# A 2D Fourier transform and an MLP in one kernel: the sequence transform multiplies plain float32 instead of high and low halves

## The chip, the cores and the metric

The kernel runs on one core of a Trainium2 chip. Its engines work side by side, each through a queue of its own: TensorE (PE, matrix products; its weight loads are shown apart as PEld), VectorE (DVE), ScalarE (ACT), GpSimd (POOL) and SyncE (SP, which here only issues transfers). Products land in PSUM, an accumulator memory, and VectorE or ScalarE read it out into SBUF, the working memory. The metric is device time of one execution in microseconds; less is better.

## The reference

```python
def _attn_ref(x):                       # x: (8, 3008, 256) float32
    X = np.fft.fft(x, axis=1)
    X = np.fft.fft(X, axis=2)
    return X.real.astype(np.float32)

def _moe_ref(x, w_in, w_out, s, b):     # x: (24064, 256), w_in: (256, 2048), w_out: (2048, 256)
    h = x @ w_in
    r = np.maximum(h, 0.0)
    g = s * (r * r) + b
    return (g @ w_out).astype(np.float32)
```

The real part of a 2D transform of each of eight samples goes, row by row, through a two-layer MLP whose activation is the square of a ReLU.

## The kernel before

**Two ways to multiply.** Most products take float32r operands, a rounded form of float32. The kernel gets its accuracy back by splitting a float32 operand into a high half (rounded to float32r by ScalarE, "h") and a low half (the rest, by VectorE or GpSimd, "l") and adding three products: high by high, low by high, high by low. A plain float32 product needs no halves; the kernel uses it where it folds the feature transform into `w_in` (L337, L345). In the trace every float32 matmul stands as two records, each with its own weight load.

**The sequence transform** (`transform(su, ph)`, L567 to L669) runs once for each sample `su` and each parity `ph`. VectorE folds the rows of x into `cs` (`load`), builds small inputs `lf` (`leaves_x`, `leaves_y`), and TensorE multiplies them by tables `dft_sb` in four pairs (leaf 0, 2, 4, 6; `pair`, L598). ScalarE makes the high halves `fh` (L576), VectorE the low halves `fl` (L579). Of a pair the result stands in an `ab` buffer of PSUM. From the second sample on, a product with the high data runs over both table halves at once (192 columns) and one with the low data over 96, so that two halves of the sum stand side by side in PSUM: VectorE copies one out (L605), adds the other (L606), and then works on from SBUF. For sample 0 the three products accumulate in PSUM, and ScalarE copies one result out (L618, `two`) so that a VectorE operation has one operand from PSUM and the other from SBUF. Sums and differences (`both`, L610 and L611) follow, and `store` splits the outcome into `spec_h` (ScalarE, L563) and `spec_l` (GpSimd, L565).

**The MLP** works in blocks of 502 columns, three for each sample, and 16 steps for each block: 384 steps. The first layer of a step is six matmuls into an `ab` buffer (L678). VectorE reads it with three operations (L680 to L682) into `h`, ScalarE applies ReLU and square and casts the result to `gh` (L683, L684, L691), GpSimd makes `gl` (L694). The second layer is twelve matmuls (L711) into four `po` banks.

**The shared buffers.** `ps_ab` has two buffers, used by the first layer and by the pairs alike. A matmul group that wants a buffer waits until the last reader of the buffer's former content is through.

**What sets the order.** The program is written out one short letter at a time and every engine keeps that order (`_in_order`, L236). START (L50) covers the weights, sample 0 and the transforms of sample 1; BATCH (L59) covers 48 steps of one sample and the two transforms of the next, and is run six times with transforms. In BATCH `L` is a first layer with its VectorE, ScalarE and GpSimd work, `S` a second layer, `l` a half of a load, `v` and `o` the next piece of the transforms of parity 0 and 1. A piece ends at a `yield`: the matmuls of a pair are one piece, and reading them out is the next. Whatever a piece issues on ScalarE thus stands behind the ReLU, the square and the cast of every `L` before it.

The row of x at feature 128 is handled apart (`nyquist`, L477): the same tables with 16 weight columns.

Of the kernel before, what the change touches and what calls it, by code (L numbers as in the profile page):

```python
# [37 lines left out]

# [4 lines left out]
COPIES_ON_SCALAR = ()  # L43
# [14 lines left out]
)  # L58
BATCH = (  # L59
# [3 lines left out]
)  # L63

# [62 lines left out]
def _dft_tables():  # L127
# [91 lines left out]
def _lay_out_x(x):  # L219

    rows, swap = _rows()
    padded = np.zeros((NB, S + 1, D), np.float32)
    padded[:, :S] = x
    first = np.arange(P)
    second = np.concatenate([[0], D - np.arange(1, P)])
    order = np.stack([np.concatenate([first, second]), np.concatenate([second, first])])
    xq = np.ascontiguousarray(padded[:, rows[..., None], order[swap]])  # L230
# [20 lines left out]
def kernel(ctx: ExitStack, tc: tile.TileContext, xq, xn, dft, turn, feat, w_in, w_out, s, b, out):  # L251
# [109 lines left out]
    dft_sb = const.tile([R, 2, 2, 8, 2, NL], F32R, name="dft_sb")  # L361
# [49 lines left out]
    def nyquist(ph, t, room, room_r):  # L411

        if ph == 0:
# [23 lines left out]
        def table(leaf, count):  # L437

            return lambda part: dft_sb[:, ph, 0, leaf, part].rearrange("p (r g) -> p r g", r=4)[
                :, :, None].broadcast_to((R, 4, count, G))  # L440

        def pairs(leaf):
            return lambda part: dft_sb[:, ph, 0, leaf, part].rearrange("p (r m) -> p r m", r=2)

        def one(leaf):
            return lambda part: dft_sb[:, ph, 0, leaf, part]

        def twice(moving, *shape):
            return lambda part: moving(part)[:, None].broadcast_to((R, 2) + shape)
# [24 lines left out]
        for i, (dst, leaf, signs, moving) in enumerate(work):  # L474
            h, l = (e_[:, leaf, signs:signs + 2].rearrange("p n b -> p (n b)") for e_ in (eh, el))
            for n, (st, part) in enumerate(((h, 0), (h, 1), (l, 0))):
                nc.tensor.matmul(dst, st, moving(part), start=i == n == 0, stop=i == len(work) - 1 and n == 2)  # L477
# [89 lines left out]
    def transform(su, ph):  # L567
# [4 lines left out]
        def halve(src):  # L572
            fh = fold.tile([R, 4, 2 * P], F32R, name="fh")
            fl = fold.tile([R, 4, 2 * P], F32R, name="fl")
            for at, v in src:
                nc.scalar.copy(fh[:, at], v)  # L576
            yield fh, fl
            for at, v in src:
                sub(fl[:, at], v, fh[:, at].bitcast(F32))  # L579
            yield  # L580

        def pair(leaf, f):

            fh, fl = f
            parts = 1 if su == 0 else 2
            ps = two_banks()[:, :, :2 * parts * NL].rearrange("p k (i h g) -> p k i h g", i=2, h=parts)
            for kind in range(2):
                at = slice(kind * P, (kind + 1) * P)
                for i in range(2):
                    tab = dft_sb[:, ph, kind, leaf + i]  # L590
                    h, l = (v[:, leaf % 4 + i, at] for v in (fh, fl))
                    if su == 0:
                        work = (ps[:, kind, i, 0], h, tab[:, 0]), (ps[:, kind, i, 0], h, tab[:, 1])
                    else:
                        work = (ps[:, kind, i], h, tab),
                    work += (ps[:, kind, i, parts - 1], l, tab[:, 0]),
                    for n, (dst, st, moving) in enumerate(work):
                        nc.tensor.matmul(dst, st, moving, start=n == 0, stop=n == len(work) - 1)  # L598
# [7 lines left out]
            add(l, l, ps[:, :, :, 0])  # L606
            return t, l
# [28 lines left out]
        t, l = yield from pair(2, f)  # L636
# [9 lines left out]
        lf = small.tile([R, 4, 2 * P], F32, name="lf", tag="tmp")  # L646
# [5 lines left out]
        g = halve([(slice(0, 4), lf)])  # L652
        f = next(g)
        yield
        next(g)
# [159 lines left out]
    def second():  # L818
# [11 lines left out]
        "n": nyquist(0, t_ny, room, room_r), "m": nyquist(1, t_ny, room, room_r),  # L830
# [62 lines left out]
```

## Time and profile before

| | |
|---|---|
| time, median of 3 runs (lowest to highest) | 1713.73 us (1713.5 to 1713.96) |
| span of the profiled execution, first to last instruction | 1711.8 us |
| what lies around that span, by the median | 1.9 us |
| PE busy, share of the span | 1675.4 us, 98% |
| PEld busy | 1382.8 us, 81% |
| DVE busy | 1395.7 us, 82% |
| ACT busy | 1284.3 us, 75% |
| POOL busy | 934.7 us, 55% |
| mean granted TensorE clock | 0.997 |

The engines overlap, so the busy times do not add up to the span. The engine with the largest share, here TensorE, sets the time only as long as nothing makes it wait; what an operation of another engine costs is decided by whether TensorE is held by it.

### The profile page before, as it was taken

How to read it: one execution, taken by the hardware profiler on the slowest of the kernel's cores; microseconds unless marked ns; L12 is line 12 of the kernel's file. 1: busy time of each engine (PE TensorE's matmuls, PEld its weight loads, DVE VectorE, ACT ScalarE, POOL GpSimd, SP SyncE). 2: the span in 40 equal slices, each digit the busy share in tenths (PEclk: the TensorE clock that was granted, in tenths of full speed). 3: DMA queues.
4: the chain of work that ended last, by engine and by line, in shares of the span. 5: the costliest groups of instructions: out<-in, count | busy, mean ns of one | idle time of the engine just before them, and what ended most of it. 6: DMA issues, size and time to landing. Idle time of an engine off the chain costs nothing.

```text
span 1711.8 us, 21668 instructions
## 1 busy us (share of the span) xinstructions
PE 1675.4 (98%) x7585; PEld 1382.8 (81%) x7585; DVE 1395.7 (82%) x2119; ACT 1284.3 (75%) x1357; POOL 934.7 (55%) x562
## 2 busy tenths in 40 slices
PE   4899999999999999999999999999999999999998
PEld 3678888788888888888888888888888888888887
DVE  7888989898778978799787997879878897875454
ACT  3877777677787777877877778777878777787776
POOL 5545555555555455655556556555565555565554
PEclk9899999999999999999999999999999999999999
DMA  7421201120001100021000200002000110000000
GB/s 184 111 63 59 67 19 31 31 74 30 1 30 46 60 31 2 29 77 29 31 7 34 77 25 25 31 25 71 23 18 30 44 43 31 1 31 29 2 24 25
DMA packets 25570, 68.56 MB, mean 40 GB/s; under 512 B 4915, under 2 KB 9875, under 8 KB 25366
## 3 DMA queue, kind: packets, MB, share of 16 engines
q1 hardware_dynamic: 24934, 64.83, 12.3%
q0 software_dynamic: 528, 2.36, 0.6%
q8 instruction: 59, 0.97, 0.2%
q14 instruction: 49, 0.40, 0.1%
HBM read 42.45 MB, written 24.73 MB: 39 GB/s over the span
## 4 chain that ended last, share of the span: by engine, by line
PE 92%; DVE 5%; ACT 1%; DMA 1%; issue 1%; POOL 0%; SPq 0%; DVEq 0%; ACTq 0%; POOLq 0%
PE po L711 59%; PE ab L678 29%; PE ab L598 3%; DVE h L680 1%; DVE h L681 1%; PE ab L337 1%; DMA raw<-in_w_in 1%; DVE h L682 1%; PE ab L477 0%; DVE xt L511 0%; DVE cs L516 0%; POOL gl L694 0%; ACT h L684 0%; ACT h L683 0%; DVE fl L579 0%
## 5 line engine op out<-in xcount | busy, mean ns | idle before, releaser
L694 POOL TENSOR_TENSOR gl<-h,gh 128x1004 fp32r<-128x1004 f32 x373 | 818.1, 2193 | 708.2 <-ACT gh L691 486.3
L683 ACT ACTIVATE h<-h 128x1004 f32<-128x1004 f32 x384 | 400.3, 1042 | 351.3 <-DVE h L682 340.1
L711 PE MATMUL po<-gh,wo_h 128*128 128x502 f32 (+1 forms) x1536 | 480.5, 393 | 0.2
L711 PE MATMUL po<-gl,wo_h 128*128 128x502 f32 (+1 forms) x1536 | 475.5, 391 | 0.5 <-POOL gl L694 0.4
L711 PE MATMUL po<-gh,wo_l 128*128 128x502 f32 (+1 forms) x1536 | 475.6, 391 | 0.0
L680 DVE SCALAR_TENSOR_TENSOR h<-ebc,wny,ab 128x502 f32<-128x502 f32 x384 | 281.3, 733 | 236.5 <-PE ab L678 224.0
L684 ACT ACTIVATE h<-h 128x1004 f32<-128x1004 f32 x384 | 401.2, 1045 | 12.2
L691 ACT CAST gh<-h 128x1004 fp32r<-128x1004 f32 x384 | 397.4, 1035 | 12.6 <-PE po L711 0.3
L711 PEld LDWEIGHTS po<-gl,wo_h 128*128 128x128 f32 x1536 | 290.5, 189 | 61.4 <-POOL gl L694 2.0
L711 PEld LDWEIGHTS po<-gh,wo_l 128*128 128x128 f32 x1536 | 289.1, 188 | 61.3
L711 PEld LDWEIGHTS po<-gh,wo_h 128*128 128x128 f32 x1536 | 286.7, 189 | 60.0 <-DVE o L734 3.3
L678 PE MATMUL ab<-spec_h,wd_h 128*128 128x502 f32 x768 | 303.5, 395 | 7.0 <-ACT spec_h L563 3.7
L678 PE MATMUL ab<-spec_h,wd_l 128*128 128x502 f32 x768 | 300.3, 391 | 0.0
L678 PE MATMUL ab<-spec_l,wd_h 128*128 128x502 f32 x768 | 299.6, 390 | 0.4 <-POOL spec_l L565 0.4
L682 DVE TENSOR_TENSOR h<-h,ab 128x502 f32<-128x502 f32 x384 | 260.6, 679 | 13.3
L681 DVE TENSOR_TENSOR h<-h,ab 128x502 f32<-128x502 f32 x384 | 260.2, 678 | 13.2
L678 PEld LDWEIGHTS ab<-spec_h,wd_h 128*128 128x128 f32 x768 | 145.9, 190 | 42.5 <-DVE h L682 9.0
L678 PEld LDWEIGHTS ab<-spec_l,wd_h 128*128 128x128 f32 x768 | 146.0, 190 | 29.6 <-POOL spec_l L565 0.9
L678 PEld LDWEIGHTS ab<-spec_h,wd_l 128*128 128x128 f32 x768 | 144.9, 189 | 30.1
L598 PE MATMUL ab<-dft_sb,fh 96*128 96x192 f32 (+1 forms) x288 | 65.8, 306 | 18.4 <-ACT fh L576 18.4
L734 DVE TENSOR_SCALAR o<-po,sb_s,bias 128x502 f32<-128x502 f32 (+1 forms) x95 | 69.2, 792 | 9.8 <-PE po L711 9.8
L511 DVE TENSOR_TENSOR xt<-xt 96x512 f32<-96x512 f32 x56 | 72.6, 1296 | 0.0
(101 smaller groups left out, 950.8 us busy)
## 6 DMA issues: line engine op xcount, KB each, us to landing
xt<-in_xq SPq DMA_DIRECT2D x64, 384.0 KB
out<-o SPq DMA_DIRECT2D x46, 502.0 KB
raw<-in_w_in SPq DMA_DIRECT2D x8, 512.0 KB
raw<-in_w_out SPq DMA_DIRECT2D x8, 512.0 KB
ebc<-e_dram SPq DMA_DIRECT2D x16, 251.0 KB
dft_sb<-in_dft POOLq DMA_DIRECT2D x2, 576.0 KB, 10.1
dft_sb<-in_dft POOLq DMA_DIRECT2D x1, 1152.0 KB, 7.3
ebc<-e_dram SPq DMA_DIRECT2D x8, 126.0 KB
```

The source lines that it names most:

```text
L511: add(t[:, 0::2], t[:, 0::2], t[:, 1::2])
L598: nc.tensor.matmul(dst, st, moving, start=n == 0, stop=n == len(work) - 1)
L678: nc.tensor.matmul(ps[:, kind], w[:, kind, fj], m[:, kind], start=i == 0, stop=i == 2)
L680: nc.vector.scalar_tensor_tensor(h[:, 0], ebc, wny[:, j:j + 1], ps[:, 0], op0=ALU.mult, op1=ALU.add)
L681: sub(h[:, 1], h[:, 0], ps[:, 1])
L682: add(h[:, 0], h[:, 0], ps[:, 1])
L683: nc.scalar.activation(h, h, AF.Relu)
L684: nc.scalar.activation(h, h, AF.Square)
L691: nc.scalar.copy(gh[:, :, :NT], h)
L694: engine.tensor_sub(gl[:, :, :NT], h, gh[:, :, :NT].bitcast(F32))
L711: nc.tensor.matmul(po[2 * pm + dh][:, :n], l[:, j, dh * P:(dh + 1) * P], r[:, pm, :n], start=start and first, stop=stop and last,)
L734: nc.vector.tensor_scalar(dst, src, *args, ALU.mult, ALU.add)
```

## The change

The tables are stored once, as float32, and the pairs and the Nyquist rows multiply float32 data by float32 tables: one matmul where there were two (samples 1 to 7) or three (sample 0 and Nyquist rows). The halves `fh`, `fl`, `eh`, `el` and the pieces that made them are gone, and with them one or two letters of each transform in START and BATCH (all other letters keep their order). The copy and the sum of PSUM halves (L605, L606) are gone too. Every sample now reads a pair the way sample 0 did: `two` copies one of the two results out on ScalarE, and `both` reads the other from PSUM. That holds for two pairs of parity 0 (leaf 0 and 6) and all four of parity 1; the other two pairs of parity 0 are read by `both` directly. The `ab` buffer of a pair is therefore free once the ScalarE copy and the two VectorE operations behind it are through. `lf` moves to a pool with one buffer.

```diff
-    return np.ascontiguousarray(np.stack([hi, v - hi], axis=4))
+    return np.ascontiguousarray(out.astype(np.float32))
...
-    dft_sb = const.tile([R, 2, 2, 8, 2, NL], F32R, name="dft_sb")
+    dft_sb = const.tile([R, 2, 2, 8, NL], F32, name="dft_sb")
...
-            h, l = (e_[:, leaf, signs:signs + 2].rearrange("p n b -> p (n b)") for e_ in (eh, el))
-            for n, (st, part) in enumerate(((h, 0), (h, 1), (l, 0))):
-                nc.tensor.matmul(dst, st, moving(part), start=i == n == 0, stop=i == len(work) - 1 and n == 2)
+            nc.tensor.matmul(
+                dst, signed[:, leaf, signs:signs + 2].rearrange("p n b -> p (n b)"), moving, start=i == 0,
+                stop=i == len(work) - 1,
+            )
...
-        def halve(src):
-            fh = fold.tile([R, 4, 2 * P], F32R, name="fh")
-            fl = fold.tile([R, 4, 2 * P], F32R, name="fl")
-            for at, v in src:
-                nc.scalar.copy(fh[:, at], v)
-            yield fh, fl
-            for at, v in src:
-                sub(fl[:, at], v, fh[:, at].bitcast(F32))
-            yield
-
-        def pair(leaf, f):
-
-            fh, fl = f
-            parts = 1 if su == 0 else 2
-            ps = two_banks()[:, :, :2 * parts * NL].rearrange("p k (i h g) -> p k i h g", i=2, h=parts)
+        def pair(leaf, data):
+
+            ps = two_banks()[:, :, :2 * NL].rearrange("p k (i g) -> p k i g", i=2)
             for kind in range(2):
                 at = slice(kind * P, (kind + 1) * P)
                 for i in range(2):
-                    tab = dft_sb[:, ph, kind, leaf + i]
-                    h, l = (v[:, leaf % 4 + i, at] for v in (fh, fl))
-                    if su == 0:
-                        work = (ps[:, kind, i, 0], h, tab[:, 0]), (ps[:, kind, i, 0], h, tab[:, 1])
-                    else:
-                        work = (ps[:, kind, i], h, tab),
-                    work += (ps[:, kind, i, parts - 1], l, tab[:, 0]),
-                    for n, (dst, st, moving) in enumerate(work):
-                        nc.tensor.matmul(dst, st, moving, start=n == 0, stop=n == len(work) - 1)
-            yield
-            t = small.tile([P, 2, 4 * NL], F32, name="t", tag="tmp")
-            if su == 0:
-                return t, ps[:, :, :, 0]
-            l = t[:, :, :2 * NL].rearrange("p k (i g) -> p k i g", i=2)
-            on_scalar = 4 * ph + leaf // 2 in COPIES_ON_SCALAR
-            (nc.scalar.copy if on_scalar else nc.vector.tensor_copy)(l, ps[:, :, :, 1])
-            add(l, l, ps[:, :, :, 0])
-            return t, l
+                    nc.tensor.matmul(ps[:, kind, i], data[i][:, at], dft_sb[:, ph, kind, leaf + i])
+            yield
+            return small.tile([P, 2, 4 * NL], F32, name="t", tag="tmp"), ps
...
         def two(t, l):
 
-            if su > 0:
-                return l[:, :, 0], l[:, :, 1]
             second = t[:, :, :NL]
             nc.scalar.copy(second, l[:, :, 1])
             return l[:, :, 0], second
...
-        lf = small.tile([R, 4, 2 * P], F32, name="lf", tag="tmp")
+        lf = fold.tile([R, 4, 2 * P], F32, name="lf")
```

Two places show how the change moves instructions. In the rows the number behind a name counts buffers; it differs between the two programs.

**Place 1** is the first pair of parity 0 in the third run of BATCH. On VectorE before, the pair's result (`ab_6720`) is copied and summed right behind the three operations of the step ahead (`h_6710`):

```order
L680 SCALAR_TENSOR_TENSOR h_6710<-ebc_6302,wny_91,ab_6703 128x502
L681 TENSOR_TENSOR h_6710<-h_6710,ab_6703 128x502
L682 TENSOR_TENSOR h_6710<-h_6710,ab_6703 128x502
L605 COPY t_6741<-ab_6720 128x2x192
L606 TENSOR_TENSOR t_6741<-t_6741,ab_6720 128x2x192
L610 TENSOR_TENSOR t_6741<-t_6741 128x2x4x24
L611 TENSOR_TENSOR t_6741<-t_6741 128x2x4x24
L680 SCALAR_TENSOR_TENSOR h_6753<-ebc_6302,wny_91,ab_6746 128x502
```

No ScalarE row touches the pair. On ScalarE now, the same pair (`ab_6385`) is copied behind the ReLU, square and cast of the step ahead (`h_6375`, `gh_6381`):

```order
L623 ACTIVATE h_6375<-h_6375 128x1004
L624 ACTIVATE h_6375<-h_6375 128x1004
L631 CAST gh_6381<-h_6375 128x2x502
L566 COPY t_6402<-ab_6385 128x2x96
L623 ACTIVATE h_6413<-h_6413 128x1004
```

and on VectorE now the first two readers of the pair take that copy (`t_6402`) as an operand, and the next step (`h_6413`) stands behind them:

```order
L620 SCALAR_TENSOR_TENSOR h_6375<-ebc_5973,wny_91,ab_6368 128x502
L621 TENSOR_TENSOR h_6375<-h_6375,ab_6368 128x502
L622 TENSOR_TENSOR h_6375<-h_6375,ab_6368 128x502
L560 TENSOR_TENSOR t_6402<-ab_6385,t_6402 128x2x4x24
L561 TENSOR_TENSOR t_6402<-ab_6385,t_6402 128x2x4x24
L620 SCALAR_TENSOR_TENSOR h_6413<-ebc_5973,wny_91,ab_6406 128x502
L621 TENSOR_TENSOR h_6413<-h_6413,ab_6406 128x502
L622 TENSOR_TENSOR h_6413<-h_6413,ab_6406 128x502
L560 TENSOR_TENSOR x_6263<-t_6402,ab_6423 128x8x48
```

What moved: reading the pair out now passes through ScalarE's queue. The next pair (`ab_6423`, leaf 2) takes the same buffer as `ab_6385`, and TensorE reaches it one second layer and one first layer (`ab_6406`) later.

**Place 2** is the last pair of parity 0 in the same run (`ab_6741`, leaf 6), whose reading stands behind the step issued after it (`h_6753`). VectorE now:

```order
L622 TENSOR_TENSOR h_6753<-h_6753,ab_6746 128x502
L560 TENSOR_TENSOR t_6763<-ab_6741,t_6763 128x2x96
L561 TENSOR_TENSOR t_6763<-ab_6741,t_6763 128x2x96
L560 TENSOR_TENSOR o_6767<-x_6263,t_6763 128x4x96
L561 TENSOR_TENSOR o_6767<-x_6263,t_6763 128x4x96
L349 SCALAR_TENSOR_TENSOR lf_6779<-cs_5758,turn_sb_87 96x256 x2
L620 SCALAR_TENSOR_TENSOR h_6801<-ebc_6497,wny_91,ab_6794 128x502
L621 TENSOR_TENSOR h_6801<-h_6801,ab_6794 128x502
L622 TENSOR_TENSOR h_6801<-h_6801,ab_6794 128x502
```

VectorE before, at the same place:

```order
L682 TENSOR_TENSOR h_7113<-h_7113,ab_7106 128x502
L605 COPY t_7123<-ab_7097 128x2x192
L606 TENSOR_TENSOR t_7123<-t_7123,ab_7097 128x2x192
L610 TENSOR_TENSOR t_7123<-t_7123 128x2x96
L611 TENSOR_TENSOR t_7123<-t_7123 128x2x96
L610 TENSOR_TENSOR o_7128<-x_6592,t_7123 128x4x96
L611 TENSOR_TENSOR o_7128<-x_6592,t_7123 128x4x96
L367 SCALAR_TENSOR_TENSOR lf_7140<-cs_6087,turn_sb_87 96x256 x2
L680 SCALAR_TENSOR_TENSOR h_7166<-ebc_6847,wny_91,ab_7159 128x502
```

ScalarE now:

```order
L623 ACTIVATE h_6753<-h_6753 128x1004
L624 ACTIVATE h_6753<-h_6753 128x1004
L631 CAST gh_6759<-h_6753 128x2x502
L566 COPY t_6763<-ab_6741 128x2x96
L540 CAST spec_h_6706<-o_6767 128x2x124
```

What moved: two VectorE operations are gone, and the four behind them, with the step `h_6801`, follow a ScalarE copy that follows the cast of `h_6753`. Behind the first layer that `h_6801` reads (`ab_6794`), TensorE has a second layer, a first layer, and directly behind that one more first layer, which takes the buffer of `ab_6794`.

More of the change, by code (lines that the diff above doesn't have):

```diff
@@ L42 @@
 X_ON_VECTOR = (0, 1, 2, 3, 5, 6, 7)
-COPIES_ON_SCALAR = ()
 SUMS_ON_SCALAR = ()
@@ L172, in _dft_tables @@
                 rotated(4 + 2 * i, 5 + 2 * i, mq[i].reshape(1, NL), sg4, 376, _unit(half, H)[0])
-    v = out.astype(np.float32)
-    bits = v.view(np.uint32)
-    hi = ((bits + 0x7FF + ((bits >> 12) & 1)) & np.uint32(0xFFFFF000)).view(np.float32)
-    return np.ascontiguousarray(np.stack([hi, v - hi], axis=4))
+    return np.ascontiguousarray(out.astype(np.float32))
 def _turn_table():
@@ L409, in nyquist_rows, with nyquist @@
         nc.gpsimd.tensor_sub(t[:, :, 3], t[:, :, 0], t[:, :, 2])
-    def nyquist(ph, t, room, room_r):
+    def nyquist(ph, t, room):
         if ph == 0:
@@ L418, in nyquist @@
         signed = room[:R, 512:832].rearrange("p (i n b) -> p i n b", i=8, b=NB)
-        eh, el = (
-            room_r[:R, i * 320:(i + 1) * 320].rearrange("p (i n b) -> p i n b", i=8, b=NB) for i in range(2)
-        )
         nc.gpsimd.tensor_copy(lf[:, :2], cs[:, :2])
@@ L427, in nyquist @@
             nc.scalar.activation(signed[:, :, n], lf, AF.Copy, scale=sign)
-        nc.scalar.copy(eh, signed)
-        yield
-        sub(el, signed, eh.bitcast(F32))
         yield
@@ L437, in table @@
         def table(leaf, count):
-            return lambda part: dft_sb[:, ph, 0, leaf, part].rearrange("p (r g) -> p r g", r=4)[
+            return dft_sb[:, ph, 0, leaf].rearrange("p (r g) -> p r g", r=4)[
                 :, :, None].broadcast_to((R, 4, count, G))
         def pairs(leaf):
-            return lambda part: dft_sb[:, ph, 0, leaf, part].rearrange("p (r m) -> p r m", r=2)
+            return dft_sb[:, ph, 0, leaf].rearrange("p (r m) -> p r m", r=2)
         def one(leaf):
-            return lambda part: dft_sb[:, ph, 0, leaf, part]
+            return dft_sb[:, ph, 0, leaf]
         def twice(moving, *shape):
-            return lambda part: moving(part)[:, None].broadcast_to((R, 2) + shape)
+            return moving[:, None].broadcast_to((R, 2) + shape)
         def last(r):
@@ L622, in by_residue @@
             return v.rearrange("p k (r g) -> p k r g", r=4)
-        lf = small.tile([R, 4, 2 * P], F32, name="lf", tag="tmp")
+        lf = fold.tile([R, 4, 2 * P], F32, name="lf")
         leaves_x(ph, cs, lf[:, 2:])
-        g = halve([(slice(0, 2), cs[:, :2]), (slice(2, 4), lf[:, 2:])])
-        f = next(g)
         yield
-        next(g)
-        yield
-        t, l = yield from pair(0, f)
+        t, l = yield from pair(0, [cs[:, i] for i in range(2)])
         x0 = t[:, :, 2 * NL:].rearrange("p k (r a g) -> p k r a g", r=4, a=2)
@@ L635, in transform @@
         yield
-        t, l = yield from pair(2, f)
+        t, l = yield from pair(2, [lf[:, i] for i in (2, 3)])
         if ph == 0:
@@ L644, in transform @@
         yield
-        lf = small.tile([R, 4, 2 * P], F32, name="lf", tag="tmp")
+        lf = fold.tile([R, 4, 2 * P], F32, name="lf")
         uv = small.tile([R, 4, 2 * P], F32, name="uv", tag="tmp")
@@ L651, in transform @@
         next(y_inputs)
[L652 to L655, printed above, removed]
         yield
         for i in range(2):
-            t, l = yield from pair(4 + 2 * i, f)
+            t, l = yield from pair(4 + 2 * i, [lf[:, 2 * i + n] for n in range(2)])
             if ph == 0 and i == 0:
@@ L745 @@
     room = spec.tile([P, 2 * NT], F32, name="room", tag="spec_h")
-    room_r = spec.tile([P, 2 * NT], F32R, name="room_r", tag="spec_l")
     t_ny = room[:R, 256:512].rearrange("p (c q b) -> p c q b", c=8, q=4)
@@ L765, in tables @@
         for ph, leaves in ((0, slice(0, 4)), (0, slice(4, 8)), (1, slice(0, 8))):
-            nc.gpsimd.dma_start(dft_sb[:, ph, :, leaves], dft[:, ph, :, leaves].bitcast(F32R))
+            nc.gpsimd.dma_start(dft_sb[:, ph, :, leaves], dft[:, ph, :, leaves])
             yield
@@ L829 @@
         "b": go_on(), "e": go_on(), "f": go_on(), "w": fold_weights(),
-        "n": nyquist(0, t_ny, room, room_r), "m": nyquist(1, t_ny, room, room_r),
+        "n": nyquist(0, t_ny, room), "m": nyquist(1, t_ny, room),
         "s": transform(0, 0), "u": transform(0, 1), "l": load(1),
```

20 rows, old and new, of tables (BATCH, START) are left out of this document.

## The prediction

> **What bounds the kernel now.** I read the page first, for the engine that is always busy, and then the view of waits for TensorE, to see whether anything holds it.
>
> ```profile
> PE 1675.4 (98%) x7585; PEld 1382.8 (81%) x7585; DVE 1395.7 (82%) x2119; ACT 1284.3 (75%) x1357; POOL 934.7 (55%) x562
> ...
> PE ab L598 <- ACT fh L576: 18.4, 1, 18.4
> ...
> PE ab L678 <- DVE h L682: 3.2, 5, 1.1
> ```
>
> TensorE is the bound. It waits once at the start (18.4 us until the first halves are there), and afterwards almost never: the costliest later wait is for a buffer that VectorE still reads (L682), 3.2 us in all. So two things can change the time: TensorE's own work, and a wait that the old order does not have. A faster VectorE by itself is worth nothing behind the start.
>
> **TensorE's own work.** The nearest rows to a plain float32 product of 96 columns are L337 (float32, 512 columns), L345 (float32, one column) and the pairs as they stand.
>
> ```profile
> 902.67 0.19 PEld L598 LDWEIGHTS ab<-dft_sb,fh 96*128 96x128 f32 x1
> ...
> 903.34 0.19 PEld L678 LDWEIGHTS ab<-spec_h,wd_h 128*128 128x128 f32 x1
> ...
> 35.57 0.19 PEld L337 LDWEIGHTS ab<-aux,feat_sb 128*128 128x128 f32 x1 [0.24 <-issue]
> 36.00 0.19 PEld L337 LDWEIGHTS ab<-aux,feat_sb 128*128 128x128 f32 x1 [0.24 <-issue]
> ...
> 36.86 1.75 PEld L345 LDWEIGHTS po<-feat_sb,aux 128*128 128x128 f32 x15 [0.24 <-issue]
> 38.53 0.30 PEld L598 LDWEIGHTS ab<-dft_sb,fh 96*128 96x128 f32 x2
> ```
>
> In a pair of today six weight loads take 903.34 − 902.67 = 0.67 us, 0.112 us each: the loads set the pace, not the columns. L345 passes fifteen loads in 38.53 − 36.86 = 1.67 us, 0.111 each, and every float32 matmul is two records with a load each. The columns of a float32 record take 36.00 − 35.57 = 0.43 us for 512, so 0.08 for 96, less than the 0.11 of the next load: by these rows the loads set the pace here too. A pair of samples 1 to 7 has eight loads now (four high, four low) and eight after (four matmuls, two records each): 0.89 us either way, no gain. Sample 0 has twelve loads in a pair and gets eight: over its second transform, four pairs, 16 × 0.11 = 1.8 us less.
>
> The Nyquist rows go from three records for each product to two. If a record costs its load, that is 2/3 of the time; if it costs its columns, a float32 record takes 0.43 us over 512, against 1675.4 / 7585 = 0.22 for the mean record of the program (mostly 502 columns), so twice as long, and the sum is 4/3. I take the dearer.
>
> ```profile
> 20.69 1.21 DVE fl L579 x2
> ...
> 27.98 4.48 PE ab L477 x36
> ...
> 89.06 3.19 PE ab L477 x45
> ```
>
> The first (4.48 us, on the chain of the start) costs 1.5 more, the second 1.1 more (by loads 1.5 and 1.1 less). Against it, the chain of the start loses two low halves (1.21 us) and some time of a table transfer that is halved; I take 0.5 for that (between 0 and 3). In sum for start and sample 0: −1.8 + 1.5 + 1.1 − 1.2 − 0.5 = −0.9, call it −1; bounds −4 (Nyquist rows by their loads, and some of the start's later halves count) and +2 (only the Nyquist rows do).
>
> **What VectorE and ScalarE gain.**
>
> ```profile
> L579 DVE TENSOR_TENSOR fl<-lf,fh 96x1024 fp32r<-96x1024 f32 x16 | 29.9, 1868 | 5.0 <-ACT fh L576 5.0
> L618 ACT COPY t<-ab 128x192 f32<-128x192 f32 x6 | 1.8, 308 | 4.9 <-PE ab L598 4.9
> L610 DVE TENSOR_TENSOR t<-ab,t 128x192 f32<-128x192 f32 x6 | 2.1, 352 | 1.2 <-ACT t L618 1.1
> ```
>
> These engines lose the halves and the PSUM sums, tens of microseconds, all under TensorE's cover, so worth 0. What they get is the last two rows, six times for each of samples 1 to 7: a ScalarE copy of 0.31 us and a VectorE operation that needs it. Cheap by itself. The question is when the copy can start.
>
> **Place 1: the buffer of leaf 0 in parity 0, once in each BATCH.** The copy stands behind the square and cast of the step ahead.
>
> ```profile
> 801.66 0.68 DVE L682 TENSOR_TENSOR h<-h,ab 128x502 f32<-128x502 f32 x1
> ...
> 802.84 0.55 DVE L606 TENSOR_TENSOR t<-t,ab 128x384 f32<-128x384 f32 x1
> ...
> 804.89 0.25 PE L598 MATMUL ab<-dft_sb,fh 96*128 96x192 f32 x1
> ...
> 805.87 1.03 ACT L691 CAST gh<-h 128x1004 fp32r<-128x1004 f32 x1
> ```
>
> Today the buffer is free at 803.39 and TensorE takes it at 804.89: 1.5 us to spare. After, the cast has to end first (806.90 as it stands), then the copy (0.31), two VectorE operations (0.62 together) and three hand-overs (0.04 each): 807.95, and TensorE stands for 3.1 us. That is the upper bound, since ScalarE sheds two casts before this point. The lower bound: the step's three VectorE operations end at 802.34 and its three ScalarE operations take 3.18 when nothing is ahead of them (851.13 to 854.31 below), so the cast ends at 805.52 at the earliest, the buffer is free at 806.57, 1.7 us late. I take the middle, **2.4**.
>
> **Place 2: leaf 6 of parity 0, once in each BATCH.**
>
> ```profile
> 850.36 0.68 DVE L682 TENSOR_TENSOR h<-h,ab 128x502 f32<-128x502 f32 x1
> ...
> 852.13 0.36 DVE L610 TENSOR_TENSOR t<-t 128x192 f32<-128x192 f32 x1
> ...
> 853.84 0.87 DVE L367 SCALAR_TENSOR_TENSOR lf<-cs,turn_sb 96x256 f32<-96x256 f32 x2
> 854.63 0.73 DVE L680 SCALAR_TENSOR_TENSOR h<-ebc,wny,ab 128x502 f32<-128x502 f32 x1
> ...
> 856.10 0.68 DVE L682 TENSOR_TENSOR h<-h,ab 128x502 f32<-128x502 f32 x1
> ...
> 851.13 1.04 ACT L683 ACTIVATE h<-h 128x1004 f32<-128x1004 f32 x1 [1.72 <-DVE h L682]
> ...
> 853.28 1.03 ACT L691 CAST gh<-h 128x1004 fp32r<-128x1004 f32 x1
> ...
> 856.84 0.49 PE L678 MATMUL ab<-spec_h,wd_h 128*128 128x502 f32 x1
> ```
>
> Here ScalarE starts the moment the step's VectorE work ends (851.04), so there is no backlog that could shrink. VectorE, which now goes on at once, has to stand until 854.31 + 0.31 + 0.08 = 854.70. Behind the wait stand the sums of `t` and `o`, the next transform's first operations, and the next step: 2.50 us (852.13 to 854.63) and then 2.15 (854.63 to 856.78). The step that ends at 856.78 today ends at 859.35, and the first layer that starts 0.06 behind it (856.84) starts **2.55** later. Bounds 2.2 and 2.7: every duration in it is measured; what may differ is the hand-overs.
>
> The other ScalarE copies of a BATCH (parity 1) clear by the same reckoning with less than a microsecond to spare; I count nothing for them, and up to 0.8 a BATCH in the upper bound. Six runs: 6 × (2.4 + 2.55) = 29.7, bounds 6 × 3.9 = 23 and 6 × 6.6 = 40.
>
> **START, sample 1's transforms.** The same copies under another order of letters; for each a ScalarE cast that must end, and the matmul that then needs the buffer.
>
> ```profile
> 256.69 1.04 ACT L691 CAST gh<-h 128x1004 fp32r<-128x1004 f32 x1
> ...
> 260.25 0.50 PE L678 MATMUL ab<-spec_h,wd_h 128*128 128x502 f32 x1
> ...
> 271.63 1.03 ACT L691 CAST gh<-h 128x1004 fp32r<-128x1004 f32 x1
> ...
> 270.72 0.46 PE L678 MATMUL ab<-spec_h,wd_h 128*128 128x502 f32 x1
> ...
> 276.81 1.04 ACT L691 CAST gh<-h 128x1004 fp32r<-128x1004 f32 x1
> ...
> 276.25 0.40 PE L678 MATMUL ab<-spec_h,wd_h 128*128 128x502 f32 x1
> ...
> 302.03 1.03 ACT L691 CAST gh<-h 128x1004 fp32r<-128x1004 f32 x1
> ...
> 301.40 0.46 PE L678 MATMUL ab<-spec_h,wd_h 128*128 128x502 f32 x1
> ...
> 311.85 1.04 ACT L691 CAST gh<-h 128x1004 fp32r<-128x1004 f32 x1
> ...
> 315.39 0.40 PE L678 MATMUL ab<-spec_h,wd_h 128*128 128x502 f32 x1
> ```
>
> Cast end plus 1.01 (copy, two operations, hand-overs) against the matmul: 272.66 + 1.01 − 270.72 = 2.95; 277.85 + 1.01 − 276.25 = 2.6; 303.06 + 1.01 − 301.40 = 2.7, less 1.87 for a low half (its row above) that no longer stands ahead of these steps on VectorE, 0.8. The first and last go the way of place 2: 257.73 + 0.39 + 2.50 + 2.15 + 0.06 − 260.25 = 2.6; the last lacks the next transform's two operations (0.87): 312.89 + 0.39 + 1.63 + 2.15 + 0.06 − 315.39 = 1.7. Sum 10.7, bounds 8 (if ScalarE's relief counts at each) and 14 (no relief, and one more small wait).
>
> **The sum.** −1 + 29.7 + 10.7 = 39.4 on the profiled span of 1711.8, which with the 1.9 us around it is the median, 1713.7: **1753 us**; bounds 1713.7 − 4 + 23 + 8 = 1741 and 1713.7 + 2 + 40 + 14 = 1770.
>
> **Rivals.** *The copies find ScalarE empty (other side).* If the shed casts drained ScalarE's queue before each copy, TensorE would not stand, and only the start would count: between −4 and +2, about 1712. For place 1 this decides if the cast ends before 803.8 (804.89 less 1.1), 3.1 earlier than today; against it stands the lower bound of 805.52, set by TensorE's own first layer. Place 2 has no backlog to drain. Chance 0.11.
>
> *A float32 pair costs more than its loads.* If the two passes of 96 columns did not hide the next load, a record would take 0.11 plus its 0.08, or at worst twice the 0.11; 7 × 2 × 4 = 56 pairs of samples 1 to 7 would each take up to 0.9 more, 50 us: about 1803. L337 shows no load hidden behind short columns, L345 shows it, but over one column. Chance 0.07.
>
> *The waits slow TensorE's clock.*
>
> ```profile
> 41.30:44.70 3.40, 3.40 (x5) 1.33 (x5) 3.33 (x7) 1.23 (x2) 1.29 (x1) 0.50 0.36 121
> 44.70:51.50 6.80, 3.16 (x17) 2.07 (x15) 4.52 (x10) 3.08 (x7) 3.07 (x3) 1.00 0.53 167
> 51.50:58.30 6.80, 6.30 (x14) 4.49 (x15) 5.28 (x8) 5.90 (x12) 5.94 (x8) 0.50 0.16 45
> ```
>
> Behind a stretch with 3.64 us idle (44.7 to 51.5) the granted clock is 0.50 for 6.8 us. If each of the 17 waits took half a clock for 3.4 us, that is 1.7 each and 29 in all: 1782. The waits forecast here are shorter than that idle time, so I give it 0.12. The Trainium skill, "TensorE: Matmul & The Clock Gate" (Part 1, The HAM clock gate), puts the fall behind one idle window of about 3.4 us and asks for no gaps beyond about 3; by that rule waits of 1.7 to 3.1 mostly leave the clock alone, and the trace's one example agrees with it.
>
> **Chances.** Forecast 0.70 (own range 1741 to 1770), copies hidden 0.11, slow clock 0.12 (a few slow stretches still end in the range), dear pairs 0.07. Two microseconds in a thousand are about what a measurement of this kernel tells from no change. Slower has forecast, clock and pairs, 0.89; the hidden case splits into same 0.06 and faster 0.05. The range 1735 to 1784 reaches to the slow clock and leaves out the hidden case and the dear pairs, 0.18.
>
> **What would show it.** In the profile of the changed kernel TensorE's waits should name the new VectorE operations behind a pair and the step behind them, some 17 of them of 1 to 3 us, two in each BATCH; the distance of two BATCH runs should grow by 5; pairs should still take 0.9. VectorE's idle time should be put down to the ScalarE copy. The forecast is wrong if those waits are missing, if the clock falls below 0.98, or if a pair takes well over 1 us.

## The result, and the profile after

The changed kernel takes **1800.87 us** (median of four runs, 1792.28 to 1804.53) against 1713.62 us: a ratio of **1.0498** (95% interval 1.0468 to 1.0528), 87 us slower. The forecast was 1753, the range 1735 to 1784; the direction was right, but the forecast loss of 39 us is less than half of what happened.

The page of the changed kernel's profile has a span of 1790.2 us. Its line of busy times, and from the view of waits the lines for TensorE (who waits <- for what: us in total, times, longest). Line numbers differ between the kernels: L555 multiplies the pairs here, L618 is the first layer, L620 to L622 its reading by VectorE, L560 and L561 the sums and differences (`both`), L566 the ScalarE copy, L631 the cast and L634 `gl`. In the experiments on this kernel these numbers are one to five higher.

```profile
PE 1697.7 (95%) x7526; PEld 1388.3 (78%) x7526; DVE 1281.8 (72%) x1957; ACT 1258.8 (70%) x1349; POOL 927.2 (52%) x562
```

```profile
PE ab L618 <- DVE h L622: 37.7, 26, 3.4
PE ab L555 <- DMA dft_sb<-in_dft: 13.9, 1, 13.9
PE ab L555 <- DVE t L561: 13.8, 6, 2.3
...
PE ab L618 <- DVE t L561: 5.1, 4, 2.1
```

VectorE lost 114 us of work and ScalarE 26, and TensorE now waits for VectorE. The six waits of L555 for `t` are place 1, once in each BATCH; the 26 of L618 for `h` hold place 2 and more. Before, the waits of first layers for `h` came to 3.2 us (L682).

VectorE itself waits for the copy. In the view of waits for VectorE:

```profile
DVE t L560 <- ACT t L566: 139.4, 36, 5.1
```

**Place 1** in the changed kernel, in the timeline (start, duration, engine and line, idle time ahead of it and what ended it):

```profile
624.58 1.03 ACT L631 CAST gh<-h 128x1004 fp32r<-128x1004 f32 x1
625.51 0.31 ACT L566 COPY t<-ab 128x192 f32<-128x192 f32 x1
...
625.86 0.36 DVE L560 TENSOR_TENSOR t<-ab,t 128x192 f32<-128x192 f32 x1 [4.25 <-ACT t L566]
626.13 0.35 DVE L561 TENSOR_TENSOR t<-ab,t 128x192 f32<-128x192 f32 x1
...
626.63 0.54 PE L555 MATMUL ab<-dft_sb,lf 96*128 96x96 f32 x3 [2.29 <-DVE t L561]
```

Cast, copy, sum, difference, pair: the chain that was forecast, and 2.29 us of idle TensorE where 2.4 was forecast.

**Place 2**, in the same BATCH:

```profile
675.13 1.03 ACT L631 CAST gh<-h 128x1004 fp32r<-128x1004 f32 x1
676.07 0.31 ACT L566 COPY t<-ab 128x192 f32<-128x192 f32 x1
676.25 2.16 POOL L634 TENSOR_TENSOR gl<-h,gh 128x1004 fp32r<-128x1004 f32 x1 [2.83 <-ACT gh L631]
676.42 0.36 DVE L560 TENSOR_TENSOR t<-ab,t 128x192 f32<-128x192 f32 x1 [3.53 <-ACT t L566]
...
677.14 1.68 DVE L560 TENSOR_TENSOR o<-x,t 128x384 f32<-128x384 f32 x1
...
678.74 0.54 DVE L561 TENSOR_TENSOR o<-x,t 128x384 f32<-128x384 f32 x1
...
680.00 0.72 DVE L620 SCALAR_TENSOR_TENSOR h<-ebc,wny,ab 128x502 f32<-128x502 f32 x1
...
682.20 0.50 PE L618 MATMUL ab<-spec_h,wd_h 128*128 128x502 f32 x1 [3.40 <-DVE h L622]
```

The chain is the forecast one with one row out of size. The sum `o<-x,t` takes 1.68 us here and the difference right behind it, of the same shape, 0.54. It starts while GpSimd computes `gl`, which began 0.18 us after the copy and ends at 678.41; the sum ends 0.41 us behind that. The groups of such sums, first of before and then of the changed kernel (times it ran | busy us, mean ns), show that this is no single case:

```profile
L610 DVE TENSOR_TENSOR o<-x,t 128x384 f32<-128x384 f32 x31 | 18.8, 607 | 2.9 <-POOL spec_l L565 1.0
```

```profile
L560 DVE TENSOR_TENSOR o<-x,t 128x384 f32<-128x384 f32 x24 | 36.1, 1506 | 2.4 <-POOL spec_l L542 1.0
```

The cast that lets the ScalarE copy go also lets GpSimd's `gl` go. In the changed kernel all 18 such sums of the six BATCH runs, three in each, start while a `gl` runs, and take 1.68 to 1.80 us. Before, one of 31 did (2.08 us); the other 30 took 0.56.

**The clock.** The view of windows shows busy time in stretches of time (from:to, length, then busy us of PE, PEld, DVE, ACT, POOL with the number of instructions, then the granted clock as a share of full speed, then two DMA figures). In the trace the clock changes only at the edges of pieces of 3.41 us, so these are the stretches taken here:

```profile
677.24:680.66 3.42, 1.56 (x7) 0.99 (x6) 3.42 (x5) 1.00 (x3) 1.97 (x3) 1.00 0.02 5
680.66:684.07 3.41, 1.87 (x8) 1.59 (x9) 3.27 (x6) 1.85 (x2) 1.21 (x2) 1.00 0.00 0
684.07:687.48 3.41, 3.41 (x16) 2.81 (x16) 2.15 (x4) 3.31 (x5) 2.03 (x1) 1.00 0.00 0
892.28:895.70 3.42, 0.84 (x4) 0.37 (x2) 3.39 (x6) 1.00 (x3) 1.97 (x4) 1.00 0.00 0
895.70:902.52 6.82, 6.01 (x14) 4.81 (x15) 4.81 (x8) 5.10 (x5) 2.63 (x2) 0.50 0.00 0
```

The first three rows and the last two are place 2, in the second and the third BATCH run. In the second the wait is cut in two by the edge at 680.66, each piece idle for 1.5 to 1.9 us, and the clock stays. In the third 2.58 of 3.42 us fall into one piece, and the clock is 0.50 for the next 6.82 us.

The distance from one BATCH run to the next puts sizes to it (time between the starts of first layers 57 + 48r, worked out from the weight loads in each trace; the rows below the second are the experiments of the next section):

```
kernel                      distances of the six BATCH runs with transforms, us
before                      205.7 204.6 204.7 204.6 204.7 204.7
changed                     216.4 212.8 217.0 218.8 212.7 217.3
all copies on VectorE       205.4 204.0 204.0 204.0 204.0 204.0
only place 1 on ScalarE     209.5 208.1 208.1 208.1 208.0 208.0
only place 2 on ScalarE     210.5 210.3 209.2 208.9 210.1 209.2
place 2, GpSimd kept away   209.4 209.1 208.1 208.1 208.1 208.1
only parity 1 on ScalarE    209.4 206.5 206.6 206.5 206.5 206.5
old products, places 1, 2   216.2 217.7 215.2 215.1 215.2 215.2
VectorE delay of 2.9 us     206.7 205.4 205.4 205.4 206.3 205.3
VectorE delay of 4.1 us     209.5 208.1 208.1 208.1 208.1 206.5
```

In the changed kernel the second and fifth, in which the clock stays at 1.00, are 8.1 us longer than before; the other four are 11 to 14 us longer. Of the 78.4 us between the two profiled spans, 66 lie in these six runs, 11.6 ahead of them and 0.7 behind. The four runs of the changed kernel differ as their clock does (0.987 in the profiled one of 1792.28 us, 0.975 in the two of 1804.5).

### The profile page after: what moved, and what is told of

It reads as the page before. It is cut to its first block, busy times and chain, and to the rows that moved or that the text cites. A ratio compares the mean times of both kernels' runs of the same rounds, so it can differ in the third digit from the quotient of the medians.

```text
span 1790.2 us, 21386 instructions
## 1 busy us (share of the span) xinstructions
PE 1697.7 (95%) x7526; PEld 1388.3 (78%) x7526; DVE 1281.8 (72%) x1957; ACT 1258.8 (70%) x1349; POOL 927.2 (52%) x562
## 4 chain that ended last, share of the span: by engine, by line
PE 69%; DVE 17%; ACT 8%; issue 4%; DMA 1%; POOL 0%; SPq 0%; DVEq 0%; ACTq 0%; POOLq 0%
PE po L651 44%; PE ab L618 22%; DVE h L620 3%; DVE h L621 3%; ACT h L624 3%; ACT h L623 3%; DVE h L622 3%; PE ab L555 2%; ACT gh L631 2%; DVE xt L488 2%; DVE cs L493 1%; PE ab L319 1%; DVE o L674 1%; DVE xt L490 1%; DVE o L560 1%
## 5 line engine op out<-in xcount | busy, mean ns | idle before, releaser
L634 POOL TENSOR_TENSOR gl<-h,gh 128x1004 fp32r<-128x1004 f32 x373 | 811.7, 2176 | 758.2 <-ACT gh L631 482.4
L620 DVE SCALAR_TENSOR_TENSOR h<-ebc,wny,ab 128x502 f32<-128x502 f32 x384 | 281.2, 732 | 299.1 <-PE ab L618 286.2
L651 PE MATMUL po<-gh,wo_h 128*128 128x502 f32 (+1 forms) x1536 | 487.0, 398 | 3.0 <-DVE o L674 3.0
L631 ACT CAST gh<-h 128x1004 fp32r<-128x1004 f32 x384 | 397.2, 1034 | 18.5 <-PE po L651 6.4
L618 PE MATMUL ab<-spec_h,wd_h 128*128 128x502 f32 x768 | 307.1, 400 | 47.2 <-DVE h L622 37.7
L651 PEld LDWEIGHTS po<-gh,wo_l 128*128 128x128 f32 x1536 | 293.2, 191 | 62.8
L651 PEld LDWEIGHTS po<-gh,wo_h 128*128 128x128 f32 x1536 | 290.3, 191 | 62.1 <-ACT gh L631 3.5
L618 PE MATMUL ab<-spec_l,wd_h 128*128 128x502 f32 x768 | 301.6, 393 | 0.3 <-POOL spec_l L542 0.3
L618 PE MATMUL ab<-spec_h,wd_l 128*128 128x502 f32 x768 | 300.5, 391 | 0.0
L622 DVE TENSOR_TENSOR h<-h,ab 128x502 f32<-128x502 f32 x384 | 260.4, 678 | 13.2
L618 PEld LDWEIGHTS ab<-spec_h,wd_h 128*128 128x128 f32 x768 | 146.6, 191 | 94.8 <-DVE h L622 52.9
L618 PEld LDWEIGHTS ab<-spec_h,wd_l 128*128 128x128 f32 x768 | 145.8, 190 | 29.4
L618 PEld LDWEIGHTS ab<-spec_l,wd_h 128*128 128x128 f32 x768 | 146.8, 191 | 27.5 <-POOL spec_l L542 0.6
L560 DVE TENSOR_TENSOR t<-ab,t 128x192 f32<-128x192 f32 x48 | 17.1, 356 | 139.6 <-ACT t L566 139.4
L542 POOL TENSOR_TENSOR spec_l<-o,spec_h 128x368 fp32r<-128x368 f32 (+3 forms) x80 | 62.0, 796 | 51.4 <-ACT spec_h L540 50.8
L540 ACT CAST spec_h<-o 128x368 fp32r<-128x368 f32 (+3 forms) x80 | 31.5, 441 | 70.9 <-DVE o L561 70.6
```

The costliest lines, as they stand in the source:

```text
L542: nc.gpsimd.tensor_sub(lo, src, hi.bitcast(F32))
L618: nc.tensor.matmul(ps[:, kind], w[:, kind, fj], m[:, kind], start=i == 0, stop=i == 2)
L620: nc.vector.scalar_tensor_tensor(h[:, 0], ebc, wny[:, j:j + 1], ps[:, 0], op0=ALU.mult, op1=ALU.add)
L622: add(h[:, 0], h[:, 0], ps[:, 1])
L631: nc.scalar.copy(gh[:, :, :NT], h)
L634: engine.tensor_sub(gl[:, :, :NT], h, gh[:, :, :NT].bitcast(F32))
```

## The experiments

The theory to be tested: the loss is the place of the PSUM copy in ScalarE's queue, in three parts (TensorE's waits at places 1 and 2 and behind parity 1, a VectorE sum held by GpSimd, half a clock behind a long enough wait). The rival: the float32 products themselves, or the letters without low halves, cost the time.

**All copies of samples 1 to 7 on VectorE.** `COPIES_ON_SCALAR` in these kernels lists the pairs (4 × parity + leaf / 2) whose copy stays on ScalarE.

```diff
+COPIES_ON_SCALAR = ()
...
-        def two(t, l):
+        def two(t, l, leaf):
...
-            nc.scalar.copy(second, l[:, :, 1])
+            on_scalar = su == 0 or 4 * ph + leaf // 2 in COPIES_ON_SCALAR
+            (nc.scalar.copy if on_scalar else nc.vector.tensor_copy)(second, l[:, :, 1])
```

> The changed kernel with its six copies of samples 1 to 7 on VectorE in place of ScalarE; the float32 products stay. If the loss comes from a copy that stands behind ReLU, square and cast on ScalarE (theory A), TensorE's waits behind a pair fall back to almost nothing, a BATCH takes its old 204.6 us and the time is 1709 to 1714 us. If the float32 products or the order of letters without the low-half pieces cost the time (rival B), it stays above 1740 us.

Measured: **1706.05 us**, ratio to before 0.9956 (0.9942 to 0.9971), clock 0.998. The view of waits for TensorE from the first BATCH on has one line left:

```profile
PE ab L620 <- DVE h L624: 1.1, 1, 1.1
```

The whole loss is gone with the engine of the copy, and what is left of the change is a gain of 7.6 us. The rival falls, for this kernel has the float32 products and the order without low halves. A BATCH is at 204.0, 0.65 below before: in the timeline of weight loads, small waits of the old order for VectorE (0.46 and 0.21 us for `o`, L734, and 0.27 for `h`, L682, in the second BATCH) are gone too. VectorE pays 0.353 us for such a copy (L568, 42 of them), ScalarE 0.31.

**One place at a time.** `COPIES_ON_SCALAR = (0,)` for place 1, `(3,)` for place 2, `(4, 5, 6, 7)` for parity 1.

> Only the copy of leaf 0 in parity 0 (place 1) is on ScalarE. Theory A: one wait of 2.3 us in each BATCH, six of them, and 2 to 3 us in START: 1712 + 14 + 2 = 1728 us, with up to 8 us more if some of the waits bring the clock down as in the changed kernel (2 of 6 there, some 4 us each): 1728 to 1736. Rival B: as the first run, whatever engine copies.

Measured: 1731.41 us, ratio 1.0097 (1.0080 to 1.0114). Every BATCH is 4.1 us longer than with VectorE copies, and the waits from 500 to 1560 us are these:

```profile
PE ab L556 <- DVE t L562: 11.5, 5, 2.3
```

So 2.3 us of each 4.1 are the wait. The rest is in the windows at the wait of the second BATCH:

```profile
602.10:605.51 3.41, 1.10 (x8) 0.71 (x6) 1.27 (x3) 2.06 (x3) 2.50 (x2) 1.00 0.00 0
605.51:608.92 3.41, 3.41 (x13) 2.89 (x12) 3.36 (x6) 1.88 (x2) 0.73 (x1) 0.50 0.00 0
```

2.31 us idle in one piece, then one piece of 3.41 us at half the clock, which costs half of it, 1.7: 2.3 + 1.7 = 4.0. Half the clock followed all six waits.

> Only the copy of leaf 6 in parity 0 (place 2) is on ScalarE. Theory A with VectorE's sum of x and t held by GpSimd: 3.5 us in each BATCH, six of them, and 2.5 us in START: 1712 + 21 + 2.5 = 1735 us, and up to 18 more from the clock (4 of 6 dips there): 1735 to 1753. As predicted (2.55 each, no clock): 1712 + 15.3 + 2.5 = 1730.

Measured: 1743.23 us, ratio 1.0173 (1.0158 to 1.0188), inside the theory's numbers and 13 us above the 1730 that the prediction's price gives. The waits from 520 to 1560 us:

```profile
PE ab L620 <- DVE h L624: 17.6, 6, 3.4
```

Five of them are place 2, 3.4 us each, and half the clock follows each, as it does in the BATCH ahead of this window.

**GpSimd kept away from place 2.** As the kernel with place 2 alone, and:

```diff
-        engine.tensor_sub(gl[:, :, :NT], h, gh[:, :, :NT].bitcast(F32))
+        if su >= 1 and (blk, j) == (2, 7):
+            nc.gpsimd.memset(gl[:, :, :NT].bitcast(F32), 0.0)
+        else:
+            engine.tensor_sub(gl[:, :, :NT], h, gh[:, :, :NT].bitcast(F32))
```

> As the run with place 2 alone, but in the step ahead of that copy GpSimd writes zeros into gl in place of h - gh (the low half of one step in 48 is left out), so that it reads no SBUF while VectorE adds x and t. If GpSimd's read is what stretches that sum from 0.56 to 1.7 us, the sum takes 0.56 again, the wait at place 2 falls by 1.1 to about 2.4 us, and the time is 7 us or more below the run with place 2 alone: 1727 to 1735. If the sum is slow for another reason, nothing changes.

Measured: 1735.66 us, ratio 1.0129 (1.0114 to 1.0144), 7.6 us below the run with place 2 alone. The timeline at place 2, first with place 2 alone and then with the memset:

```profile
653.78 2.17 POOL L636 TENSOR_TENSOR gl<-h,gh 128x1004 fp32r<-128x1004 f32 x1 [2.83 <-ACT gh L633]
653.96 0.36 DVE L561 TENSOR_TENSOR t<-ab,t 128x192 f32<-128x192 f32 x1 [3.53 <-ACT t L568]
...
654.68 1.68 DVE L561 TENSOR_TENSOR o<-x,t 128x384 f32<-128x384 f32 x1
...
659.75 0.79 PE L620 MATMUL ab<-spec_h,wd_h 128*128 128x502 f32 x1 [3.41 <-DVE h L624]
```

```profile
650.70 0.94 POOL L637 MEMSET gl<- 128x1004 f32 x1
...
653.71 0.36 DVE L561 TENSOR_TENSOR t<-ab,t 128x192 f32<-128x192 f32 x1 [3.53 <-ACT t L568]
...
654.43 0.56 DVE L561 TENSOR_TENSOR o<-x,t 128x384 f32<-128x384 f32 x1
...
658.38 0.49 PE L620 MATMUL ab<-spec_h,wd_h 128*128 128x502 f32 x1 [2.28 <-DVE h L624]
```

The memset waits for no cast and is over before the copy, so GpSimd is idle behind it. The same sum takes 0.56 us, and TensorE's wait falls by the 1.1 us. The wait that is left, 2.28, is near the forecast's 2.55. So the excess at place 2 is the `gl` that runs beside the sum. This run takes all of GpSimd's work away there; that its reading is what holds the sum, and not its writing, no run shows. The Trainium skill, "SBUF — State Buffer" (Who interferes with whom), says that VectorE and GpSimd share a pair of SBUF ports, held as an exclusive lock, and that a VectorE instruction with two SBUF inputs contends with a GpSimd instruction that reads SBUF; the rows agree (1.68 us beside `gl`, 0.56 without), and the prediction did not apply it.

**Parity 1 alone.**

> Only the four copies of parity 1 are on ScalarE, places 1 and 2 on VectorE. The prediction counted nothing for these, at most 0.8 us a BATCH: 1706 to 1711 us. If they cause the three smaller waits of the changed kernel (0.4, 0.85 and some 1.2 us in each BATCH), a BATCH takes 206 to 206.7 us and the time is 1706 + 6 x 2.4 = 1720, and 4 us more from START.

Measured: 1733.18 us, ratio 1.0115 (1.0100 to 1.0130). From the second BATCH on the theory's number holds (206.5 for 206 to 206.7, 2.5 us longer than with VectorE copies); the first BATCH is 4.0 longer, one piece at half the clock included. Between the very first first layer and the first BATCH lie 8 us more than with VectorE copies, where 4 were expected, one more piece at half the clock among them. The waits from 520 to 1560 us, none followed by half the clock:

```profile
PE ab L620 <- DVE h L624: 7.6, 10, 1.1
```

They make 1.5 of the 2.5 us in each BATCH; the other 1.0 is not traced. The timeline of the changed kernel shows where they start. The copy of leaf 6 of parity 1 stands behind a cast, and the sum behind it meets `gl`:

```profile
536.62 0.31 ACT L566 COPY t<-ab 128x192 f32<-128x192 f32 x1
536.84 2.15 POOL L634 TENSOR_TENSOR gl<-h,gh 128x1004 fp32r<-128x1004 f32 x1 [0.91 <-ACT gh L631]
...
537.62 1.79 DVE L560 TENSOR_TENSOR o<-x,t 128x384 f32<-128x384 f32 x1
...
544.08 0.50 PE L618 MATMUL ab<-spec_h,wd_h 128*128 128x502 f32 x1 [0.43 <-DVE h L622]
...
568.66 0.50 PE L618 MATMUL ab<-spec_h,wd_h 128*128 128x502 f32 x1 [1.08 <-DVE h L622]
```

VectorE works without a gap from the copy to the `h` of the first wait (0.43 us), so the 1.2 us by which the sum is longer carry over. The last wait, 1.08 us, comes 32 us behind the copy, in the stretch where VectorE folds the next sample's rows. It is absent with VectorE copies and present with parity 1 alone, so it hangs on these copies. It is not that VectorE is still late: at 551 us it sits idle for 1.46 us, waiting for TensorE. Behind that its folding meets `gl` in other places. In that BATCH one fold takes 2.38 us beside `gl`, and the same fold with VectorE copies 0.41:

```profile
558.50 2.38 DVE L493 TENSOR_TENSOR cs<-xt 96x256 f32<-96x256 f32 x1
```

```profile
529.52 0.41 DVE L494 TENSOR_TENSOR cs<-xt 96x256 f32<-96x256 f32 x1
```

The row of 2.38 us returns with parity 1 alone. This is read from the traces; no run kept `gl` away from these places.

**The old products with the copies moved.** The kernel before, with one line changed:

```diff
-COPIES_ON_SCALAR = ()
+COPIES_ON_SCALAR = (0, 3)
```

> The kernel before, with its products of halves, and only the PSUM copies of leaf 0 and leaf 6 of parity 0 (places 1 and 2) moved to ScalarE. If the copy's place in ScalarE's queue is the cause and the products are not, waits of about 3.1 us at place 1 and 4.2 us at place 2 appear, with 1.7 to 3.4 us of lost clock, in each of six BATCH runs: some 50 us, about 1765 us. If the float32 products are needed for the loss, the time stays at 1714.

Measured: **1786.80 us**, ratio 1.0426 (1.0409 to 1.0443). The waits of one BATCH (750 to 966 us):

```profile
PE ab L678 <- DVE h L682: 4.1, 1, 4.1
PE ab L598 <- DVE t L606: 2.8, 1, 2.8
```

Not one float32 product in the pairs, and a loss of 73 us: waits of 2.8 us at place 1 and 4.1 at place 2. The waits are near the expected 3.1 and 4.2. The total is 22 us above the 1765 that was written: the expectation's own pieces (six times 7.3, and the clock) make 54 to 64 us, not 50, which still leaves at least 9. All BATCH runs but the second are 10.5 us longer than before: 6.9 of waits, and 3.4 for the two pieces of 3.41 us at half the clock behind them (four such pieces in the second, which grew by 13); 7 us lie ahead of the first BATCH.

**What a wait costs in clock.** All copies on VectorE, ScalarE in no part of it, and ahead of the copy at place 1 in six BATCH runs five (or seven) copies that nobody reads:

```diff
+            if su >= 2 and ph == leaf == 0:
+                for _ in range(5):
+                    nc.vector.tensor_copy(t[:, :, 2 * NL:].rearrange("p k (i g) -> p k i g", i=2), l)
```

> All copies on VectorE, and in each of six BATCH runs five copies of the pair at place 1 that nobody reads, ahead of the real one (0.58 us each, 2.9 in all against 1.65 us of slack there). TensorE should wait 1.25 us once in each BATCH. If the clock falls only where about 2 us of one 3.4 us window are idle, it stays at 1.00 and the time is 1706 + 6 x 1.25 = 1713.5 us. If every wait costs clock, 1713.5 + 10 = 1724.

> As the run before with seven such copies, 4.06 us against 1.65: a wait of 2.4 us in each BATCH, this time with ScalarE in no part of it. By the wait alone 1706 + 14.4 = 1720.5 us; with half a clock for one window of 3.41 us behind each (1.7 us), 1706 + 24.6 = 1730.5, as with place 1 on ScalarE.

Measured: 1715.55 us with five (ratio 1.0012, 1.0003 to 1.0022) and 1733.50 us with seven (ratio 1.0114, 1.0097 to 1.0131). The waits from 380 to 1560 us, with five copies and with seven:

```profile
PE ab L556 <- DVE t L562: 7.0, 6, 1.2
```

```profile
PE ab L556 <- DVE t L562: 14.1, 6, 2.4
```

The waits doubled, by 7.1 us in all; the time grew by 18. With five the clock stays at 1.00 behind every wait, and a BATCH is 1.3 to 1.4 us longer than without a delay (one, the fifth, 2.3). With seven, five BATCH runs are 4.1 longer and one, the last, 2.5. The windows of the second and of the last:

```profile
604.18:607.59 3.41, 1.42 (x10) 1.38 (x11) 3.27 (x8) 0.92 (x1) 2.28 (x2) 1.00 0.00 0
607.59:611.01 3.42, 3.42 (x10) 2.72 (x9) 2.63 (x5) 2.08 (x2) 0.00 (x0) 0.50 0.00 0
...
1437.03:1440.44 3.41, 1.89 (x13) 1.77 (x14) 3.31 (x8) 0.44 (x1) 2.13 (x1) 1.00 0.00 0
1440.44:1443.86 3.42, 3.42 (x17) 2.82 (x16) 2.16 (x5) 3.12 (x3) 0.00 (x0) 1.00 0.00 0
```

The same wait of 2.4 us: with 1.99 us idle in one piece the clock falls, with 1.52 it does not. From the second run to the sixth the idle time of that piece shrinks in steps, 1.99, 1.86, 1.77, 1.64 and 1.52 us, and the clock falls behind all but the last.

**Sample 0's copies on VectorE too.**

```diff
-            on_scalar = su == 0 or 4 * ph + leaf // 2 in COPIES_ON_SCALAR
+            on_scalar = 4 * ph + leaf // 2 in COPIES_ON_SCALAR
```

> All PSUM copies of pairs on VectorE, those of sample 0 too (there both kernels use ScalarE). In the steady part nothing differs from the first run (BATCH 204.0 us). At the start TensorE waits 8 us for sums behind a copy (the Nyquist products) that may come earlier or later, VectorE being the busier engine there: 1706 us within 4.

Measured: 1709.06 us, ratio 0.9970 (0.9958 to 0.9982). No gain over the run that leaves sample 0 on ScalarE (0.9956, 0.9942 to 0.9971); the intervals overlap, so which of the two is better is not settled. Both take slightly less time than the kernel before (0.4% and 0.3%).

## Why the prediction was wrong

The mechanism was right: the copies stand behind the cast in ScalarE's queue, and TensorE waits. Three terms of the sum failed. Place 2 was priced too low, the copies of parity 1 were put at nothing, and the lost clock was kept out of the sum.

**What held.** A float32 pair costs its loads. In the timeline of weight loads:

```profile
626.60 0.97 PEld L555 LDWEIGHTS ab<-dft_sb,lf 96*128 96x128 f32 x8 [2.69 <-ACT t L566]
627.49 0.30 PEld L651 LDWEIGHTS po<-gh,wo_h 128*128 128x128 f32 x2
```

Eight loads in 0.89 us, as forecast, so the rival of dear pairs was wrong, though its 1803 lies nearest to the result. Place 1 was right (2.4 forecast, 2.29 measured), in its chain; that 2.4 came so close owes something to luck, for it was the middle between bounds of 1.7 and 3.1. The estimate for sample 1's transforms was right only as a sum: 10.7 forecast, and from 200 to 340 us the waits of the changed kernel are

```profile
PE ab L618 <- DVE h L622: 5.3, 3, 2.7
PE ab L618 <- DVE t L561: 5.1, 4, 2.1
```

10.4 us; the clock comes on top. Place by place, 2.6, 2.95, 2.6, 0.8 and 1.7 were forecast, and 2.26, 2.06, 1.02, 1.51 and 2.66 are in the timeline, so the misses cancelled by luck. The rival of copies that find ScalarE empty was refuted at both places. VectorE's relief, put at nothing, gains a little: the 0.65 us of each BATCH that the kernel with VectorE copies shows, 4 us in all.

**Place 2, a term that was mis-sized.** "Bounds 2.2 and 2.7: every duration in it is measured; what may differ is the hand-overs." The durations were measured in another position. The sum of `x` and `t` had 0.56 us in a gap of GpSimd's work (`gl` ended at 851.65, the next began at 854.39); moved behind the cast, it meets the `gl` that the same cast releases, and takes 1.68. The wait is 3.4 us for 2.55: 0.85 × 6 = 5 us.

**The copies of parity 1, a term put at nothing.** "Clear by the same reckoning with less than a microsecond to spare; I count nothing for them, and up to 0.8 a BATCH in the upper bound." The run with parity 1 alone shows 2.5 us in five BATCH runs and 4.0 in the first, 16.5 in all, and 8 us ahead of them (with clock). Less than a microsecond to spare was no margin: by the timeline, the sum stretched by GpSimd takes 1.2 us, and behind it folds meet `gl` that did not before.

**The clock, a rival that should have been in the sum.** It got 0.12, because "the waits forecast here are shorter than that idle time" of 3.64 us. That row showed one idle time that sufficed, not the least that does. Nor was it the trace's one example: the first row shown there has a clock of 0.50 too, and the piece ahead of it holds only 1.14 us without a matmul:

```profile
37.87:41.28 3.41, 2.27 (x21) 2.18 (x20) 1.44 (x2) 2.20 (x4) 2.82 (x6) 1.00 0.27 40
```

Waits of 2.3 us can be enough: place 1 alone lost the clock six times of six. In the changed kernel, whose waits fall differently on the pieces, four of six BATCH runs lost it, in nine pieces of 3.41 us, 15 us in all, and three pieces ahead of the first BATCH cost 5 more. The Trainium skill, "TensorE: Matmul & The Clock Gate" (HAM oscillation — how this bites in real kernels), sums its rule up as no gaps beyond about 3.4 us. Here half the clock followed waits of 2.3 us, so the measurement decides, and leaning on that rule was the mistake.

**The sum again**, on the profiled spans: 78 us. Six BATCH runs at 8.1 without loss of clock make 49. By the starts of first layers, place 1 sets a BATCH back by 2.5 us, place 2 by 3.8 and parity 1 by 2.5, less the 0.65 that the change gains; the setbacks at places 1 and 2 are 0.2 to 0.4 us longer than the idle time shown. The clock in four runs makes 15, 2 in these runs are not placed, and 12 lie outside them, 5 of these by the clock. The forecast had 30 for the BATCH runs and 10 for START. As a check, the three runs with one place each on ScalarE are 25, 37 and 27 us above the run with VectorE copies, 90 in all, and the changed kernel is 95 above it. The median of the four runs, most of them with a lower clock than the profiled one, is 87 us above before.

**What stays open**: whether the waits behind parity 1 go when `gl` is kept away (read from traces, not tested), 1.0 us of each BATCH with these copies, and whether sample 0's copies belong on VectorE or ScalarE.

## What to carry to other kernels

A readout on an in-order engine starts behind everything that was issued ahead of it there: before a PSUM copy moves to an engine with less load, look at what stands in that queue when the accumulator is full, and who holds still until the copy is done. Take a duration along only with its neighbours: two operations that one event now releases together can hold each other. And put a lost clock into the sum for a stall of TensorE as soon as it can empty some two microseconds of one 3.4 us piece; at place 1 that cost 1.7 us beside a wait of 2.3.

## What the hardware showed that was not expected

In all traces here the changes of the clock lie on a grid of 3.413 us that goes on through the run. Counted over the profiled kernels here (before, changed and all nine experiments) from 150 to 1690 us, with idle time as the piece less TensorE's busy time and a piece at full clock: all 42 pieces with at least 1.95 us idle were followed by half the clock, none of 29 with 1.0 to 1.5 us was, and of 18 in between 6 were. So the same stall costs 1.7 us more or nothing, by where an edge of the grid cuts it. Idle time by these records does not settle it alone: among the 18, one piece with 1.51 us was followed by half the clock and one with 1.92 was not, and ahead of 150 us 1.14 us sufficed (the row at 37.87 us above, a piece with many matmuls of one and of 96 columns). What decides there is open.

A kernel whose period is near a whole number of pieces keeps the same answer for many periods: with place 1 alone, 208.1 us is 60.96 pieces, and all six waits fell into one piece each. It can still drift out: with the delay of seven copies the period is the same, each wait lies some 0.13 us earlier on the grid than the last, and of the sixth too little was left in one piece. With the changed kernel's longer and uneven periods some waits were cut and some not. Its four runs spread over 12 us with clocks of 0.975 to 0.987, where those of the kernel before, in the same comparison, stay within 1; only one of the four has a trace, so how the others were cut is not shown.
